# Angles kept in SBUF until a sine pass in every third step: re-ordering a tuned recurrence-and-mixer kernel

## The chip, the cores and the metric

One core of a Trainium2 chip runs the whole program. The metric is the device time of one execution in microseconds (us). Before the change the kernel took 284.85 us, the median of 3 runs (280.71 to 285.94). A run that is more than 1.5% above the fastest of its kernel is called slow; 285.94 is one. Ratios here are of fast runs only.

The engines are named as in the profile: PE is TensorE's matmuls, PEld its weight loads, DVE is VectorE, ACT is ScalarE, POOL is GpSimd. In the traces each has its own sequence of instructions, with waits where an input is missing.

## The reference, cut to what matters

The first half is a linear recurrence with decay over 768 time steps, for 4 batches and 8 heads of 40. The second half is a mixer: angles theta, sine and cosine, a product with two 768x768 token weights, and a channel layer.

```python
for t in range(S):                                   # B, H, S, D = 4, 8, 768, 40
    y[:, :, t] = einsum('bhd,bhde->bhe', rt, state)
    Sa = einsum('bhde,bhe->bhd', state, at)
    state = state * wt[:, :, None, :] - einsum('bhd,bhe->bhde', Sa, bt) \
            + einsum('bhd,bhe->bhde', vt, kt)
x = y.transpose(0, 2, 1, 3).reshape(B, S, 320)

theta = x @ w_theta                                  # 320 x 320
zr, zi = x * cos(theta), x * sin(theta)
y = einsum('ts,bsd->btd', w_tok_r, zr) + einsum('ts,bsd->btd', w_tok_i, zi)
u = x + y
out = u + maximum(u @ w_ch, 0)
```

## The kernel before

The sequence is cut into 24 tiles of 128 time steps (4 batches of 6). One pass of the main loop is one **step**. It does the recurrence of tile i, prepares tile i+2, finishes tile i-1, and does one mixer row of an earlier batch. Names that return below:

- **nx** is the negated intermediate of the recurrence. ScalarE copies it once per step, so the times of the 24 nx copies cut the run into steps. "Nx 8" is the start of the ninth copy.
- **lw, invW, Wi** are a logarithm and two exponentials on ScalarE. They prepare a tile.
- **kb** is the **key product** (k and b times invW), **ah** is a times Wi, **rv** the casts of r and v. All three are on GpSimd, and TensorE then transposes them.
- **aT, rvT, kbT, nuT, gd, xT, uT** are copies of transposes from PSUM to SBUF.
- **z products** are x times cosine and x times sine, six per sine pass, on GpSimd.

```python
def prep_csi(i):
    ...                                              # matmul of the running log-decay
    nc.scalar.activation(out=q.invW..., in_=csi[:, 0:DM], func=AF.Exp)
    nc.gpsimd.tensor_tensor(out=q.kbh[:, :, :, 0:D], in0=q.kb,
                            in1=q.invW.to_broadcast([128, 2, H, D]), op=ALU.mult)

def prep_rv(i):
    for j in range(2):
        nc.gpsimd.tensor_copy(out=q.rvb[:, j, :, 0:D], in_=q.rv[:, j])

def moe_phase(bi, js):                               # three tiles at once
    th = tile_of(ps_sc, [128, 1024], FP32, "sc")     # one of two large PSUM buffers
    ...                                              # theta = xT * w_theta, into th
    for c in range(2):                               # cosine (bias pi/2), then sine
        tc.keep_in_program_order(nc.scalar.activation(
            out=cs[:, c, 0:n * DM], in_=th[:, 0:n * DM], func=AF.Sin,
            bias=(pi2_col[:, :], 0.0)[c]))
    ...                                              # 6 z products on GpSimd

for i in range(N):                                   # N = 24
    nxt(load, i + 4)
    nxt(prep_ln, i + 2)
    rec_x0(i)                                        # makes nx
    nxt(tr_a, i + 1)                                 # makes aT
    ...
    nxt(prep_csi, i + 2)
    rec_nu(i)
    if i > 0: out_y(i - 1)
    nxt(sc_psiphi, i + 1)                            # scores from aT and kbT
    ...
    nxt(prep_cse, i + 2)
    if i > 0: out_xt(i - 1)                          # makes xT
    nxt(prep_rv, i + 2)
    for m in yrows: moe_y(*m)                        # one mixer row
    nxt(tr_rv, i + 2); nxt(tr_kb, i + 2)
    ...
    if i < NCH: moe_wtok(i)                          # token weights, steps 0 to 5
    if i == 1: moe_weights()
    if ci == 3: moe_phase(bi, (0, 1, 2)); ln_exp_again()
    if ci == 0 and bi > 0: moe_phase(bi - 1, (3, 4, 5)); ln_exp_again()
```

In the trace each of the seven sine passes in the loop has two table loads on ScalarE, one ahead of its sines and one behind them (1.28 us each, see below; `ln_exp_again` is the second). The framework's scheduler may move any instruction that is not given to `keep_in_program_order`, so the order in the trace is not the order of this text.

## Time and profile before

| part of the run, cut by nx | us | what it is |
|---|---|---|
| start to nx 0 | 25.4 | first loads, first tiles prepared |
| nx 0 to nx 8 | 78.8 | the inputs come in |
| nx 8 to nx 23 | 143.1 | steady: 10 plain steps, 5 with a sine pass |
| nx 23 to the end | 35.5 | tail |

First, lines of the profile's page: span, busy time per engine, then the busy share of 40 equal slices of the span in tenths (PEclk is the granted clock of TensorE in tenths), and the DMA packets.

```profile
span 282.8 us, 8177 instructions
PE 219.1 (77%) x3392; PEld 174.1 (62%) x3392; DVE 183.1 (65%) x262; ACT 159.6 (56%) x294; POOL 125.2 (44%) x172
...
PEclk9999999888779999998998899979997999999979
DMA  8999999899399849827963597457410000011012
...
DMA packets 155684, 30.81 MB, mean 109 GB/s; under 512 B 150400, under 2 KB 155648, under 8 KB 155648
```

No engine is full over the whole span, so the average names no limit; the parts have to be read one by one. The DMA line shows one limit: the 16 engines are busy through the first slices. Nearly all packets are under 512 B (a head's row of 40 floats is 160 B), and the next view has all engines busy at 160 to 170 GB/s. That the size of the packets is the cause is not shown.

The windows view of the kernel before, one line per part (the input-bound part in two). Columns: window, length, busy us with number of instructions for PE, PEld, DVE, ACT, POOL, then granted clock, DMA share (1.00 is 16 busy engines), GB/s.

```profile
0.00:25.40 25.40, 8.83 (x87) 6.59 (x88) 14.57 (x43) 7.04 (x13) 12.32 (x27) 1.00 0.97 160
25.40:66.20 40.80, 31.21 (x512) 25.67 (x512) 27.74 (x35) 23.61 (x45) 19.27 (x29) 0.96 1.04 170
66.20:104.20 38.00, 26.93 (x492) 22.79 (x492) 25.17 (x31) 22.80 (x43) 23.15 (x31) 0.87 0.77 133
104.20:247.30 143.10, 126.34 (x2077) 102.14 (x2076) 104.20 (x133) 96.51 (x179) 65.87 (x81) 0.95 0.49 92
247.30:282.80 35.50, 25.78 (x229) 16.92 (x227) 11.40 (x22) 9.62 (x19) 4.57 (x6) 0.95 0.13 47
```

In the steady part PE is busy 126.34 of 143.10 us, 88%. Most of the other 12% (16.8 us) is a wait for ScalarE: 11.9 us, in the waits view further down. This is the timeline of ACT around one sine pass (start, duration, engine, line, operation, then idle time before it and what ended that):

```profile
119.69 0.46 ACT L255 ACTIVATE nx<-sm 128x320 bf16<-128x320 f32 x1
120.16 1.28 ACT L405 ACT_TABLE_LOAD   x1
121.46 1.06 ACT L405 ACTIVATE cs<-sc,pi_col 128x960 f32<-128x960 f32 x1
122.42 0.96 ACT L405 ACTIVATE cs<-sc 128x960 f32<-128x960 f32 x1
123.40 1.28 ACT L414 ACT_TABLE_LOAD   x1
124.69 0.58 ACT L182 COPY aT<-sm 128x512 bf16<-128x512 bf16 x1
```

The pass takes 4.5 us, from 120.16 to 124.69, and it stands between nx and aT. TensorE's scores need aT. All table loads of the sine passes in this trace took 1.28 us, and the first sine here starts 0.02 us after its load (120.16 + 1.28 = 121.44, start 121.46).

The second kind of hole is in the input-bound part. The timeline of POOL before, in step 4 to 5, which took 15.5 us:

```profile
70.77 0.45 POOL L126 CAST rv_104<-raw_rv 128x320 bf16<-128x320 f32 x1 [5.74 <-DMA raw_rv<-in_r_dram]
71.18 0.78 POOL L410 TENSOR_TENSOR zr<-cs,x_118 128x320 bf16<-128x320 f32 x1
...
74.92 0.78 POOL L410 TENSOR_TENSOR zi<-cs,x_122 128x320 bf16<-128x320 f32 x1
75.67 1.52 POOL L137 TENSOR_TENSOR kb_98<-raw_kb,invW 128x640 bf16<-128x640 f32 x1
```

GpSimd waits 5.74 us for a transfer of r, then does six z products, and only then the key product. Two lines of the waits view of before (engine, line, what it waited for: total us, times, longest) show what both holes cost TensorE (of the second line, the 6.2 are this hole; the rest is a wait in step 0):

```profile
PE sc L196 <- ACT aT L182: 11.9, 5, 2.7
...
PE sm L164 <- POOL kb_98 L137: 8.5, 2, 6.2
```

### The profile page before, as it was taken

Reading aid. Unit: us, or ns where it says so; the run is one execution under the profiler, and the core shown is the slowest. Engines: PE = TensorE matmul, PEld = TensorE weight load, DVE = VectorE, ACT = ScalarE, POOL = GpSimd, SP = SyncE. Lnnn points to the kernel's source line nnn. Section 1 sums busy time; section 2 is a strip of 40 time slices with the busy share of each in tenths; the row PEclk is TensorE's granted clock in tenths of the full one; section 3 lists DMA queues with packets and bytes.
Section 4 is the critical chain, followed back from the end, with each engine's and each line's share of the span. In section 5 each row is a group of like instructions: output and inputs, shape, how many; then the busy total and the mean of one; then the engine's idle time right before and its main releaser. Section 6 shows DMA issues by size and latency. Waiting matters only on the chain.

```text
span 282.8 us, 8177 instructions
## 1 busy us (share of the span) xinstructions
PE 219.1 (77%) x3392; PEld 174.1 (62%) x3392; DVE 183.1 (65%) x262; ACT 159.6 (56%) x294; POOL 125.2 (44%) x172
## 2 busy tenths in 40 slices
PE   1374698686198779969996999699969995996693
PEld 0253577475087667857775788477757875764462
DVE  7643579694069869846884788468846885752042
ACT  3243366377237986685658666956595569334121
POOL 3742546521954484464446444564445333204200
PEclk9999999888779999998998899979997999999979
DMA  8999999899399849827963597457410000011012
GB/s 136 179 182 155 189 181 161 148 170 176 65 171 166 150 77 172 158 57 123 175 123 77 96 167 140 92 94 143 87 32 2 26 26 26 1 49 49 0 46 93
DMA packets 155684, 30.81 MB, mean 109 GB/s; under 512 B 150400, under 2 KB 155648, under 8 KB 155648
## 3 DMA queue, kind: packets, MB, share of 16 engines
q1 hardware_dynamic: 153216, 27.54, 53.5%
q0 software_dynamic: 2432, 2.77, 6.2%
q8 instruction: 26, 0.43, 0.6%
q14 instruction: 10, 0.08, 0.1%
HBM read 29.13 MB, written 3.93 MB: 117 GB/s over the span
## 4 chain that ended last, share of the span: by engine, by line
PE 51%; ACT 14%; DMA 10%; DVE 8%; SPq 7%; POOL 4%; issue 4%; POOLq 0%; ACTq 0%; DVEq 0%
PE sm L420 13%; PE sm L164 9%; SPq L115 7%; DMA raw_rv<-in_r_dram 7%; PE sc L196 7%; PE sm L382 4%; ACT cs L405 3%; ACT L414 3%; DVE lamv L204 3%; PE sc L382 3%; DMA raw_rv<-in_v_dram 2%; PE sm L344 2%; PE sm L285 2%; ACT aT L182 2%; PE sc L420 2%
## 5 line engine op out<-in xcount | busy, mean ns | idle before, releaser
L204 DVE TENSOR_TENSOR psi<-sc,mask_p 128x1024 bf16<-128x1024 f32 x24 | 29.2, 1218 | 17.3 <-PE sc L196 17.3
L190 ACT COPY rvT<-sm 128x1024 bf16<-128x1024 bf16 x24 | 24.3, 1013 | 21.2 <-PE sm L164 21.2
L420 PE MATMUL sm<-zr,wtok_r 128*128 128x320 bf16 x120 | 36.0, 320 | 0.0
L420 PE MATMUL sm<-zi,wtok_i 128*128 128x320 bf16 x120 | 35.5, 316 | 0.0
L175 DVE COPY kbT<-sm 128x1024 bf16<-128x1024 bf16 x24 | 16.6, 690 | 22.4 <-PE sm L164 22.4
L204 DVE TENSOR_TENSOR phi<-sc,mask_n 128x1024 bf16<-128x1024 f32 x24 | 29.2, 1215 | 0.5 <-PE sc L196 0.5
L196 PE MATMUL sc<-aT,kbT 64*128 64x128 bf16 x384 | 19.0, 235 | 13.2 <-ACT aT L182 11.9
L204 DVE TENSOR_TENSOR lamu<-sc,mask_p 128x1024 bf16<-128x1024 f32 x24 | 29.2, 1215 | 0.0
L204 DVE TENSOR_TENSOR lamv<-sc,mask_p 128x1024 bf16<-128x1024 f32 x24 | 29.2, 1215 | 0.0
L313 ACT COPY nuT<-sm 128x512 bf16<-128x512 bf16 x24 | 14.0, 585 | 24.3 <-PE sm L164 24.3
L196 PEld LDWEIGHTS <-kbT 64*128 64x128 bf16 x384 | 13.5, 102 | 14.7 <-issue 13.5
L420 PEld LDWEIGHTS <-wtok_r 128*128 128x128 bf16 x144 | 15.0, 104 | 10.7 <-issue 4.9
L304 ACT COPY gd<-sm 128x320 bf16<-128x320 bf16 x20 | 8.5, 426 | 19.1 <-PE sm L164 19.1
L420 PEld LDWEIGHTS <-wtok_i 128*128 128x128 bf16 x144 | 14.9, 103 | 7.0 <-issue 1.2
L347 ACT COPY uT<-sm 128x384 bf16<-128x384 bf16 x24 | 11.4, 483 | 12.7 <-PE sm L344 12.7
L182 ACT COPY aT<-sm 128x512 bf16<-128x512 bf16 x24 | 14.2, 593 | 3.8 <-PE sm L164 3.7
L382 PE MATMUL sm<-wch,uT 128*128 128x320 bf16 x72 | 14.4, 315 | 2.3 <-ACT uT L347 2.3
L263 PEld LDWEIGHTS <-phi 128*128 128x128 bf16 x192 | 8.6, 97 | 11.7 <-issue 10.1
L255 ACT ACTIVATE nx<-sm 128x320 bf16<-128x320 f32 x24 | 10.8, 450 | 6.2 <-PE sm L251 6.2
L331 PEld LDWEIGHTS <-lamu 128*128 128x128 bf16 x192 | 13.1, 97 | 1.7 <-DVE lamu L204 0.7
L328 PEld LDWEIGHTS <-lamv 128*128 128x128 bf16 x192 | 13.8, 96 | 0.4 <-issue 0.4
L137 POOL TENSOR_TENSOR kb_100<-raw_kb,invW 128x640 bf16<-128x640 f32 x6 | 9.2, 1541 | 10.8 <-ACT invW L134 10.8
(324 smaller groups left out, 676.0 us busy)
## 6 DMA issues: line engine op xcount, KB each, us to landing
raw_w<-in_w_dram SPq DMA_DIRECT2D x24, 160.0 KB, 4.4
raw_kb<-in_k_dram SPq DMA_DIRECT2D x24, 160.0 KB, 3.2
raw_kb<-in_b_dram SPq DMA_DIRECT2D x24, 160.0 KB, 3.7
raw_a<-in_a_dram SPq DMA_DIRECT2D x24, 160.0 KB, 3.8
raw_rv<-in_r_dram SPq DMA_DIRECT2D x24, 160.0 KB, 4.0
raw_rv<-in_v_dram SPq DMA_DIRECT2D x24, 160.0 KB, 4.5
out_dram<-oo SPq DMA_DIRECT2D x24, 160.0 KB, 1.8
wtok_row<-in_moe_w_tok_r_dram POOLq DMA_DIRECT2D x6, 192.0 KB, 4.8
```

The lines of the kernel that those rows point to most:

```text
L115: nc.sync.dma_start(out=dst, in_=src(ap))
L164: nc.tensor.transpose(out=dst[:, g * 128:(g + 1) * 128], in_=src[:, 2 * g:2 * g + 2, :].rearrange("p a b -> p (a b)"), identity=ident)
L175: nc.vector.tensor_copy(out=q.kbT.rearrange("p a b -> p (a b)"), in_=pt)
L182: nc.scalar.copy(out=q.aT, in_=pt[:, 0:512])
L190: nc.scalar.copy(out=q.rvT.rearrange("p a b -> p (a b)"), in_=pt)
L196: nc.tensor.matmul(P[:, p, g, :], lhsT=lhs[rows(p), g * 128:(g + 1) * 128], rhs=rhs[rows(p), g * 128:(g + 1) * 128], start=True, stop=True)
L204: nc.vector.tensor_tensor(out=s.rearrange("p a b c -> p (a b) c"), in0=P.rearrange("p a b c -> p (a b) c"), in1=mask.to_broadcast([128, 2 ...
L313: nc.scalar.copy(out=q.nuT, in_=pt[:, 0:512])
L328: nc.tensor.matmul(o, lhsT=q.lamv[:, p, g, :], rhs=q.kbh[:, 0, h, 0:D], start=first, stop=False, skip_group_check=True)
L331: nc.tensor.matmul(o, lhsT=q.lamu[:, p, g, :], rhs=q.kbh[:, 1, h, 0:D], start=False, stop=True, skip_group_check=True)
L382: nc.tensor.matmul(dst, lhsT=lhs[:, kt, :], rhs=rhs[:, kt, :], start=kt == 0, stop=kt == 2)
L420: nc.tensor.matmul(yp, lhsT=wtok[nm][:, sb, j * 128:(j + 1) * 128], rhs=z[:, sb], start=start and n == 0, stop=stop and n == 2 * len(sbs) - 1)
```

## The change

The intent: theta goes to SBUF by a small copy in every step, so a sine pass no longer holds a large PSUM buffer and can stand where ScalarE has time, behind xT. In those steps the three copies that follow (rvT, gd, uT) go to VectorE. Z products come one step after their sines. The mixer's weight loads are taken out of the start and their transposes come two steps later. The first two tiles are prepared on ScalarE and VectorE instead of GpSimd. The logarithm runs three tiles ahead instead of two.

```diff
     def prep_ln(i):
-        nc.scalar.activation(out=q.lw[:, :, 0:D], in_=q.w, func=AF.Ln)
+        tc.keep_in_program_order(
+            nc.scalar.activation(out=q.lw[:, :, 0:D], in_=q.w, func=AF.Ln))
     def prep_rv(i):
         for j in range(2):
-            nc.gpsimd.tensor_copy(out=q.rvb[:, j, :, 0:D], in_=q.rv[:, j])
+            if i < 2:
+                nc.scalar.copy(out=q.rvb[:, j, :, 0:D], in_=q.rv[:, j])
+            else:
+                nc.gpsimd.tensor_copy(out=q.rvb[:, j, :, 0:D], in_=q.rv[:, j])
     def prep_csi(i):
-        nc.gpsimd.tensor_tensor(out=q.kbh[:, :, :, 0:D], in0=q.kb,
-                                in1=q.invW.to_broadcast([128, 2, H, D]),
-                                op=ALU.mult)
+        for j in range(2):
+            (nc.vector if i < 2 else nc.gpsimd).tensor_tensor(
+                out=q.kbh[:, j, :, 0:D], in0=q.kb[:, j], in1=q.invW[:, 0],
+                op=ALU.mult)
     # ... the a product likewise; copies of rvT, gd, xT and uT become
+    def evac(out, in_):
+        if busy_act[0]:
+            nc.vector.tensor_copy(out=out, in_=in_)
+        else:
+            nc.scalar.copy(out=out, in_=in_)
     # ... moe_phase is cut into three
+    def moe_theta(i):
+        tp = tile_of(ps_sm, [128, 512], FP32, "sm")
+        mix3(tp[:, 0:DM], tiles[i].xT, wth)
+        nc.scalar.copy(out=ths[bi][:, j], in_=tp[:, 0:DM])
+    # moe_z: the six z products;  moe_sines: the two sines, from ths in SBUF
     for i in range(N):
         nxt(load, i + 4)
-        nxt(prep_ln, i + 2)
         rec_x0(i)
         nxt(tr_a, i + 1)
+        if i > 1:
+            moe_theta(i - 2)
     # ...
         if i > 0:
             out_xt(i - 1)
+        due = None
+        if sines:
+            due = (bi, (0, 1, 2)) if ci == 4 else (bi - 1, (3, 4, 5))
+            moe_sines(*due)
+            ln_exp_again()
+            busy_act[0] = True
         nxt(prep_rv, i + 2)
     # ... mixer row, transposes, rec_gd, uT
+        busy_act[0] = False
+        if i == 0:
+            moe_weights()
         if i < NCH:
-            moe_wtok(i)
-        if i == 1:
-            moe_weights()
-        if ci == 3:
-            moe_phase(bi, (0, 1, 2)); ln_exp_again()
-        if ci == 0 and bi > 0:
-            moe_phase(bi - 1, (3, 4, 5)); ln_exp_again()
+            wtok_load(i)
+        if 2 <= i < NCH + 2:
+            wtok_trans(i - 2)
+        nxt(prep_ln, i + 3)
+        if z_due:
+            moe_z(*z_due)
+        z_due = due
```

(Shortened: padding is zeroed in another order, the work ahead of the loop is re-ordered, the weight loads are pinned in program order, mixer rows start one step later and catch up with two rows in each of the last three steps, and the tail uses the new pieces.)

More of the change, by code (lines that the diff above doesn't have):

```diff
@@ L62, with padded, last24 @@
     NB = 4
-    def padded(name, shape, n):
-        ts = []
-        for i in range(n):
-            t = consts.tile(shape, BF16, name=f"{name}_{i}")
-            nc.vector.memset(t, 0.0)
-            ts.append(t)
-        return ts
-    lw_t = padded("lw", [128, H, 64], 2)
-    ah_t = padded("ah", [128, H, 64], 2)
-    kb_t = padded("kb", [128, 2, H, 64], NB)
-    rv_t = padded("rv", [128, 2, H, 64], NB)
-    nu_t = padded("nu", [128, H, 64], 2)
-    gt_t = padded("gt", [128, G, 2, 64], 2)
-    x_t = padded("x", [128, 3 * 128], 2 * NCH)
-    u_t = padded("u", [128, 3 * 128], 3)
+    def padded(name, shape, n, pads):
+        ts = [consts.tile(shape, BF16, name=f"{name}_{i}") for i in range(n)]
+        for i, t in enumerate(ts):
+            to_zero.append((i, pads(t)))
+        return ts
+    to_zero = []
+    def last24(t):
+        return t[:, :, D:64] if len(t.shape) == 3 else t[:, :, :, D:64]
+    lw_t = padded("lw", [128, H, 64], 2, last24)
+    ah_t = padded("ah", [128, H, 64], 2, last24)
+    kb_t = padded("kb", [128, 2, H, 64], NB, last24)
+    rv_t = padded("rv", [128, 2, H, 64], NB, last24)
+    nu_t = padded("nu", [128, H, 64], 2, last24)
+    gt_t = padded("gt", [128, G, 2, 64], 2, last24)
+    x_t = padded("x", [128, 3 * 128], 2 * NCH, lambda t: t[:, DM:])
+    u_t = padded("u", [128, 3 * 128], 3, lambda t: t[:, DM:])
+    for i, t in sorted(to_zero, key=lambda e: e[0]):
+        nc.vector.memset(t, 0.0)
     raw = ctx.enter_context(tc.tile_pool(name="raw", bufs=3))
@@ L90 @@
     ps_sm = ctx.enter_context(tc.tile_pool(name="ps_sm", bufs=4, space=PSUM))
+    busy_act = [False]
+    def evac(out, in_):
[3 more added lines that the diff above has]
+            nc.scalar.copy(out=out, in_=in_)
     def rows(p):
@@ L157, in prep_cse @@
         q.ah = ah_t[i % 2]
-        nc.gpsimd.tensor_tensor(out=q.ah[:, :, 0:D], in0=q.a,
-                                in1=q.Wi[:, 0:DM].rearrange("p (h d) -> p h d", h=H),
-                                op=ALU.mult)
+        (nc.vector if i < 2 else nc.gpsimd).tensor_tensor(
+            out=q.ah[:, :, 0:D], in0=q.a,
+            in1=q.Wi[:, 0:DM].rearrange("p (h d) -> p h d", h=H), op=ALU.mult)
     def transpose4(dst, src):
@@ L189, in tr_rv @@
         q.rvT = tile_of(trs, [128, 2, 512], BF16, "rvT")
-        nc.scalar.copy(out=q.rvT.rearrange("p a b -> p (a b)"), in_=pt)
+        evac(out=q.rvT.rearrange("p a b -> p (a b)"), in_=pt)
     def score(lhs, rhs):
@@ L303, in rec_gd @@
         gd = tile_of(sml, [128, 8, D], BF16, "gd")
-        nc.scalar.copy(out=gd, in_=pt[:, 0:512].rearrange(
+        evac(out=gd, in_=pt[:, 0:512].rearrange(
             "p (n d) -> p n d", d=64)[:, :, 0:D])
@@ L346, in x_transpose @@
         dst = tile_of(xp, [128, 3, 128], BF16, tag)
-        nc.scalar.copy(out=dst.rearrange("p a b -> p (a b)"), in_=pt[:, 0:384])
+        evac(out=dst.rearrange("p a b -> p (a b)"), in_=pt[:, 0:384])
         return dst
@@ L354, with pool_dma, wtok_load, wtok_trans @@
     wtok = {}
+    def pool_dma(out, in_):
+        tc.keep_in_program_order(nc.gpsimd.dma_start(out=out, in_=in_))
     def moe_weights():
         for dst, src in ((wth, moe_w_theta), (wch, moe_w_ch)):
-            nc.gpsimd.dma_start(out=dst[:, 0:2, :], in_=src[0:256, :].rearrange(
+            pool_dma(out=dst[:, 0:2, :], in_=src[0:256, :].rearrange(
                 "(a p) d -> p a d", p=128))
-            nc.gpsimd.dma_start(out=dst[0:64, 2, :], in_=src[256:320, :])
+            pool_dma(out=dst[0:64, 2, :], in_=src[256:320, :])
     for nm in ("r", "i"):
         wtok[nm] = mw.tile([128, NT, S], BF16, name=f"wtok_{nm}")
-    def moe_wtok(tb):
+    wrow = ctx.enter_context(tc.tile_pool(name="wrow", bufs=3))
+    wrows = {}
+    def wtok_load(tb):
         for nm, ap in (("r", moe_w_tok_r), ("i", moe_w_tok_i)):
-            row = tile_of(mk, [128, S], BF16, "wtok_row")
-            nc.gpsimd.dma_start(out=row, in_=ap[tb * 128:(tb + 1) * 128, :])
+            row = tile_of(wrow, [128, S], BF16, f"wtok_row_{nm}")
+            pool_dma(out=row, in_=ap[tb * 128:(tb + 1) * 128, :])
+            wrows[nm, tb] = row
+    def wtok_trans(tb):
+        for nm in ("r", "i"):
             pt = tile_of(ps_sm, [128, 1024], BF16, "sm")
@@ L371, in moe_wtok @@
                 nc.tensor.transpose(out=pt[:, sb * 128:(sb + 1) * 128],
-                                    in_=row[:, sb * 128:(sb + 1) * 128],
+                                    in_=wrows[nm, tb][:, sb * 128:(sb + 1) * 128],
                                     identity=ident)
@@ L385, with moe_z, moe_sines @@
     zs = {}
-    def moe_phase(bi, js):
+    ths = {}
+    def moe_theta(i):
+        bi, j = divmod(i, NCH)
+        if bi not in ths:
+            ths[bi] = tile_of(mk, [128, NT, DM], FP32, "th")
+        tp = tile_of(ps_sm, [128, 512], FP32, "sm")
+        mix3(tp[:, 0:DM], tiles[i].xT, wth)
+        nc.scalar.copy(out=ths[bi][:, j], in_=tp[:, 0:DM])
+    cs_of = {}
+    def moe_z(bi, js):
+        cs = cs_of[bi, js[0]]
+        for m, j in enumerate(js):
+            for c in range(2):
+                nc.gpsimd.tensor_tensor(out=zs[bi][c][:, j], in0=cs[:, c, m],
+                                        in1=tiles[bi * NCH + j].x, op=ALU.mult)
+    def moe_sines(bi, js):
         if bi not in zs:
@@ L391, in moe_phase @@
                       tile_of(mk, [128, NT, DM], BF16, "zi"))
-        zr, zi = zs[bi]
-        n = len(js)
-        if n > 1:
-            th = tile_of(ps_sc, [128, 1024], FP32, "sc")
-        else:
-            th = tile_of(ps_sm, [128, 512], FP32, "sm")
-        for m, j in enumerate(js):
-            lo, hi = m * DM, m * DM + DM
-            cuts = [lo, 512, hi] if lo < 512 < hi else [lo, hi]
-            for c0, c1 in zip(cuts, cuts[1:]):
-                mix3(th[:, c0:c1], tiles[bi * NCH + j].xT, wth[:, :, c0 - lo:c1 - lo])
-        cs = tile_of(mk, [128, 2, 3 * DM], FP32, "cs")
+        j0, n = js[0], len(js)
+        cs = tile_of(mk, [128, 2, 3, DM], FP32, "cs")
+        cs_of[bi, j0] = cs
         for c in range(2):
             tc.keep_in_program_order(nc.scalar.activation(
-                out=cs[:, c, 0:n * DM], in_=th[:, 0:n * DM], func=AF.Sin,
+                out=cs[:, c, 0:n], in_=ths[bi][:, j0:j0 + n], func=AF.Sin,
                 bias=(pi2_col[:, :], 0.0)[c]))
-        for c, z in enumerate((zr, zi)):
-            for m, j in enumerate(js):
-                nc.gpsimd.tensor_tensor(out=z[:, j], in0=cs[:, c, m * DM:m * DM + DM],
-                                        in1=tiles[bi * NCH + j].x, op=ALU.mult)
     def ln_exp_again():
@@ L453, in nxt @@
             f(i)
-    def prep(i):
-        prep_ln(i)
-        prep_csi(i)
-        prep_cse(i)
     rows_at = {}
-    for s in range(NCH + 2, 3 * NCH + 2):
-        rows_at[s] = [divmod(s - NCH - 2, NCH)]
-    for s, js in ((20, (0,)), (21, (1,)), (22, (2, 3)), (23, (4, 5))):
-        rows_at[s] = [(2, j) for j in js]
+    for s in range(NCH + 3, 3 * NCH + 3):
+        rows_at[s] = [divmod(s - NCH - 3, NCH)]
+    for s in range(3):
+        rows_at[3 * NCH + 3 + s] = [(2, 2 * s), (2, 2 * s + 1)]
     for i in range(4):
         load(i)
-    prep(0)
+    prep_ln(0)
+    prep_csi(0)
+    prep_cse(0)
     tr_kb(0)
     tr_a(0)
-    prep_rv(0)
-    prep(1)
     sc_psiphi(0)
     ev_phi(0)
+    prep_rv(0)
     tr_rv(0)
+    prep_ln(1)
+    prep_csi(1)
+    prep_cse(1)
     lv = score(tiles[0].rvT[:, 1], tiles[0].rvT[:, 0])
     tiles[0].lamv = masked("lamv", lv, mask_p)
+    tr_kb(1)
     prep_rv(1)
-    tr_kb(1)
     tr_rv(1)
+    prep_ln(2)
     prev = []
+    z_due = None
     for i in range(N):
+        bi, ci = divmod(i, NCH)
         yrows = rows_at.get(i, [])
+        sines = ci == 4 or (ci == 1 and bi > 0)
         nxt(load, i + 4)
-        nxt(prep_ln, i + 2)
         rec_x0(i)
         nxt(tr_a, i + 1)
-        for m in prev:
-            moe_ch(*m)
+        if i > 1:
+            moe_theta(i - 2)
         nxt(prep_csi, i + 2)
@@ L493 @@
             out_y(i - 1)
+        nxt(prep_cse, i + 2)
         nxt(sc_psiphi, i + 1)
@@ L497 @@
         nxt(ev_phi, i + 1)
-        nxt(prep_cse, i + 2)
         if i > 0:
             out_xt(i - 1)
+        due = None
[4 more added lines that the diff above has]
+            busy_act[0] = True
+        for m in prev:
+            moe_ch(*m)
         nxt(prep_rv, i + 2)
@@ L509 @@
             moe_ut(*m)
+        busy_act[0] = False
+        if i == 0:
+            moe_weights()
         if i < NCH:
-            moe_wtok(i)
-        if i == 1:
-            moe_weights()
-        bi, ci = divmod(i, NCH)
-        if ci == 3:
-            moe_phase(bi, (0, 1, 2))
-            ln_exp_again()
-        if ci == 0 and bi > 0:
-            moe_phase(bi - 1, (3, 4, 5))
-            ln_exp_again()
+            wtok_load(i)
[5 more added lines that the diff above has]
+        z_due = due
         prev = yrows
+    moe_theta(N - 2)
+    moe_sines(B - 1, (3, 4))
+    moe_z(B - 1, (3, 4))
+    out_y(N - 1)
     for m in prev:
         moe_ch(*m)
-    moe_phase(B - 1, (3, 4))
-    out_y(N - 1)
     acc = [tile_of(ps_sc, [128, 2, 512], FP32, "sc") for _ in range(2)]
@@ L532 @@
         y_part(yps[j], B - 1, j, range(NT - 1), True, False)
-    moe_phase(B - 1, (5,))
+    moe_theta(N - 1)
+    moe_sines(B - 1, (5,))
+    moe_z(B - 1, (5,))
     for j in range(NT):
```

## The prediction

> **What bounds the kernel now.** 284.85 us (profiled span 282.8). Cut by the start of the negated-x copy (nx) on ScalarE, one per step, the run has four parts.
>
> 1. Start, to 25.4 us (timeline): the first nx stands behind the logarithm of tile 3, which waited 5.3 us for its input (25.0).
> 2. Input-bound part, nx 0 (25.4) to nx 8 (104.3). The windows view gives 16 DMA engines fully busy at 167 GB/s up to 70 us; 150,400 of 155,684 packets are under 512 B. [...] A tile is 0.98 MB, mixer rows 0.39 MB a step: about 8.1 us a step while both load, 5.9 after (estimates). Two steps take 13.9 and 15.5 us: the first holds a sine pass (61.0 to 66.1); in the second GpSimd has a cast of r, waiting 5.7 us for DMA, then six z products (4.7 us), ahead of the key product, for which TensorE and VectorE wait 7.5 us.
> 3. Steady part, nx 8 to nx 23 (247.3): plain steps 7.2 to 8.1 us, sine steps 12.5 to 13.4. Groups of three take about 28.7 us; TensorE is busy 25.3 to 25.8 of it. A sine pass is load 1.28 + sines 1.06 and 0.96 + load 1.28 = 4.6 us on ScalarE, between nx and aT, and TensorE's scores wait for aT (up to 2.7 us, waits view).
> 4. Tail, 35.5 us.
>
> [...]
>
> **The change.**
> - As many table loads. Added: 24 theta copies on ScalarE, 0.44 us each (estimate from equal-sized copies). Theta drops from 12 matmuls to 9 per three tiles and frees the large PSUM buffer.
> - The pass moves behind xT, where the rvT, gd and uT copies (1.01 + 0.43 + 0.48) go to VectorE in those steps. ScalarE's order gives nx to xT 4.5 + 0.44 + pass 4.6 + logarithm 0.48 = 10.0 us for a sine step. VectorE: 7.5 us in a plain step, about 9.0 in a sine step. Groups of 8 + 8 + 10 = 26 us, near TensorE's floor of 25.
> - z products come a step later, off the key product's way.
> - Weights are issued after the first tiles: 0.8 MB, about 4.5 us of DMA, leaves the first 20 us. Tiles 0 and 1 avoid GpSimd; tile 0's scores precede tile 1's transposes; the logarithm three tiles ahead follows gd. Nx 0 near 19.
>
> **Sum.** Start -6. Input-bound part: nx 1 near 26, then about 8 us a step with two sine steps of 10: nx 8 near 84 to 86 instead of 104.3, -19 in all by then. Steady: 15 steps in 130 instead of 143, -13. Tail: +0 to +1 (a theta copy in the last chain). Span near 251.
>
> **Predicted 253 us, 80% range 244 to 265.** Faster by over 2%: 0.95; within 2%: 0.04; slower: 0.01.
>
> **Right if:** first nx by 20 us; no step over 11 us after step 1; sine steps 9.5 to 10.5; TensorE's wait for aT at passes gone; the 7.5 us waits for a key product gone; tail 35 to 37.
>
> **Wrong if:** VectorE bounds sine steps (over 11 us); GpSimd's z products still delay keys; the theta copy stretches plain steps above 8.3; input DMA, with weights in steps 0 to 5, holds steps at 9 or more; or the granted clock falls below 0.94 [...].

The cuts are two passages and a clause that no run of this case shows. No term of the sum is among them: -19 by nx 8 (the -6 of the start included), -13 and 0 to +1 take the span from 282.8 to about 251, and the 2 us by which the 284.85 us exceed their span make it 253. Two figures in it are estimates. The 4.5 us of DMA for 0.8 MB of weights (also in the expectation of e9) would be 4.8 at the 167 GB/s that it names. The 7.5 and 9.0 us for VectorE were not measured either: in the windows view VectorE was busy 5.9 to 7.3 us in the plain steps of the steady part before, and 6.4 and 8.1 us in a plain and a sine step of the kernel after (118.0 to 126.4 and 109.1 to 118.0).

## The result, and the profile after

The kernel after took 260.64 us, the median of 4 fast runs (260.36 to 262.26). The kernel before had 283.58 (280.71 to 285.94, 4 runs); without the slow run, which is 1.9% above the lowest, the median of three is 282.30. The ratio of fast runs is 0.923, with a 95% interval of 0.914 to 0.933: faster. A ratio is the mean time of one kernel's fast runs over that of the other's of the same rounds, so it is not quite the ratio of the medians quoted.

| part, cut by nx | before | predicted | after |
|---|---|---|---|
| start to nx 0 | 25.4 | 19 | 18.7 |
| nx 0 to nx 8 | 78.8 | 65 to 67 | 74.4 |
| nx 8 to nx 23 | 143.1 | 130 | 130.3 |
| tail | 35.5 | 35.5 to 36.5 | 37.1 |
| profiled span | 282.8 | about 251 | 260.5 |

One row is off by 8 us. It is nearly the whole difference between 253 predicted and 260.6.

Lines of the page of the kernel after, the same as shown of before:

```profile
span 260.5 us, 8110 instructions
PE 215.0 (83%) x3368; PEld 167.8 (64%) x3368; DVE 185.4 (71%) x287; ACT 160.4 (62%) x303; POOL 120.9 (46%) x186
...
PEclk9999997999659979999999999999999999999778
DMA  7999999999999898767697579645500001011012
...
DMA packets 155685, 30.81 MB, mean 118 GB/s; under 512 B 150401, under 2 KB 155649, under 8 KB 155649
```

All busy shares are up because nearly the same work is done in less time. The granted clock is lowest in slices 11 and 12, at 6 and 5 tenths (the slow step below), and it is 7, 7, 8 at the end (the tail).

The windows view of the kernel after, columns as before. The third line is the step from nx 5 (61.0) to nx 6 (75.75).

```profile
0.00:18.70 18.70, 8.01 (x86) 6.66 (x87) 10.99 (x49) 8.09 (x15) 1.86 (x12) 1.00 1.05 165
18.70:61.00 42.30, 35.12 (x613) 28.06 (x613) 32.57 (x40) 28.20 (x56) 24.86 (x39) 0.96 1.01 171
61.00:75.75 14.75, 7.81 (x121) 6.15 (x121) 6.85 (x9) 4.67 (x12) 10.47 (x17) 0.70 1.07 179
75.75:93.10 17.35, 14.22 (x267) 11.38 (x266) 14.95 (x22) 13.85 (x24) 9.46 (x15) 0.96 1.02 163
93.10:223.40 130.30, 122.72 (x2060) 97.90 (x2060) 107.42 (x146) 94.82 (x181) 67.83 (x97) 0.99 0.55 102
223.40:260.50 37.10, 27.12 (x226) 17.61 (x225) 12.62 (x26) 10.82 (x21) 6.41 (x9) 0.87 0.13 45
```

In the steady part PE is now busy 122.72 of 130.30 us, 94% against 88%. As the profile models the ends of matmuls, this is no distance to a peak. It says that less waiting is left. The windows also show DMA fully busy up to nx 8 (share 1.01 to 1.07, at 163 to 179 GB/s); the busy work before that point is not what fills the time (PE is busy 65.16 of those 93.1 us).

The timeline of ACT after, around one sine pass in the steady part:

```profile
109.07 0.44 ACT L273 ACTIVATE nx<-sm 128x320 bf16<-128x320 f32 x1
...
112.54 0.48 ACT L103 COPY xT_2435<-sm 128x384 bf16<-128x384 bf16 x1
113.04 1.28 ACT L443 ACT_TABLE_LOAD   x1
114.33 1.10 ACT L443 ACTIVATE cs<-th,pi_col 128x960 f32<-128x960 f32 x1
115.34 0.99 ACT L443 ACTIVATE cs<-th 128x960 f32<-128x960 f32 x1
116.34 1.28 ACT L447 ACT_TABLE_LOAD   x1
117.63 0.47 ACT L134 ACTIVATE lw_87<-raw_w 128x320 bf16<-128x320 f32 x1
118.01 0.42 ACT L273 ACTIVATE nx<-sm 128x320 bf16<-128x320 f32 x1
```

The step is 118.01 - 109.07 = 8.9 us: 3.5 from nx to xT, 0.5 for xT, 4.6 for the pass, 0.4 for the logarithm. The first sine starts 0.01 us after its table load (113.04 + 1.28 = 114.32, start 114.33). ScalarE is without a gap from xT to the next nx, yet TensorE loses less than before, because aT is long done. It still waits for the nx behind the pass, up to 1.4 us (waits view below).

The timeline of POOL after, in the slow step, and the ScalarE line that ends it:

```profile
61.28 0.45 POOL L143 CAST rv_97<-raw_rv 128x320 bf16<-128x320 f32 x1 [2.92 <-DMA raw_rv<-in_r_dram]
...
63.63 0.82 POOL L432 TENSOR_TENSOR zr<-cs,x_102 128x320 bf16<-128x320 f32 x1
...
67.38 0.78 POOL L432 TENSOR_TENSOR zi<-cs,x_104 128x320 bf16<-128x320 f32 x1
69.47 0.45 POOL L143 CAST rv_94<-raw_rv 128x320 bf16<-128x320 f32 x1 [1.31 <-DMA raw_rv<-in_r_dram]
...
70.52 1.67 POOL L155 TENSOR_TENSOR kb_93<-raw_kb,invW 128x320 bf16<-128x320 f32 x2
```

```profile
75.75 0.44 ACT L273 ACTIVATE nx<-sm 128x320 bf16<-128x320 f32 x1 [8.98 <-PE sm L269]
```

The key product of tile 7 (70.52) had its invW at 62.9 us. It stood behind six z products and behind two casts of tile 8, whose r arrived only at 69.5. In the program's text this key product comes ahead of those casts and of those z products; the scheduler put it behind both. Of the two, the casts came last: the z products ended at 68.16, and GpSimd then still waited 1.31 us for r, whose transfer had been issued at 62.82, before the first of them. So the z products alone did not set the start of the key product in this step; the input did, for an engine that had been given a cast of tile 8 ahead of the key product of tile 7. Of the waits view of after, the lines of TensorE for this and for nx:

```profile
PE sm L182 <- POOL kb_93 L155: 6.5, 2, 6.3
...
PE sm L410 <- ACT nx L273: 7.5, 9, 1.4
```

Before, the longest wait of this kind in the input-bound part was 6.2 us. So the wait that the change was to remove has come back one step later. The line for aT, 11.9 us before, has no counterpart any more; waits for nx in the steady part, 5.9 us of the 7.5, are about half as long.

### The profile page after: what moved, and what is told of

It reads as the page before. It is cut to its first block, busy times and chain, and to the rows that moved or that the text cites. A ratio compares the mean times of both kernels' runs of the same rounds, so it can differ in the third digit from the quotient of the medians.

```text
span 260.5 us, 8110 instructions
## 1 busy us (share of the span) xinstructions
PE 215.0 (83%) x3368; PEld 167.8 (64%) x3368; DVE 185.4 (71%) x287; ACT 160.4 (62%) x303; POOL 120.9 (46%) x186
## 4 chain that ended last, share of the span: by engine, by line
PE 46%; ACT 15%; issue 12%; DMA 10%; POOL 9%; DVE 4%; SPq 3%; POOLq 0%; DVEq 0%; ACTq 0%
PE sm L453 10%; DMA raw_rv<-in_r_dram 9%; PE sm L182 7%; PE sc L214 6%; PE sm L410 5%; ACT cs L443 4%; SPq L128 3%; ACT L443 2%; ACT L447 2%; PE sc L453 2%; PE sm L362 2%; PE sm L349 2%; PE sm L278 2%; DVE lamu L222 1%; POOL kb_93 L155 1%
## 5 line engine op out<-in xcount | busy, mean ns | idle before, releaser
L103 ACT COPY rvT<-sm 128x1024 bf16<-128x1024 bf16 x18 | 18.2, 1013 | 26.0 <-PE sm L182 26.0
L453 PE MATMUL sm<-zr,wtok_r 128*128 128x320 bf16 x120 | 33.8, 304 | 0.0
L453 PE MATMUL sm<-zi,wtok_i 128*128 128x320 bf16 x120 | 33.7, 303 | 0.0
L453 PEld LDWEIGHTS <-wtok_r 128*128 128x128 bf16 x144 | 14.4, 100 | 9.6 <-issue 3.9
L273 ACT ACTIVATE nx<-sm 128x320 bf16<-128x320 f32 x24 | 10.4, 432 | 11.5 <-PE sm L269 11.5
L103 ACT COPY uT<-sm 128x384 bf16<-128x384 bf16 x18 | 8.5, 483 | 14.1 <-PE sm L362 14.1
L143 POOL CAST rv_96<-raw_rv 128x320 bf16<-128x320 f32 x12 | 5.4, 453 | 24.5 <-DMA raw_rv<-in_r_dram 21.8
L155 POOL TENSOR_TENSOR kb_93<-raw_kb,invW 128x320 bf16<-128x320 f32 x12 | 10.1, 866 | 13.2 <-ACT invW L151 13.2
L424 ACT COPY th<-sm 128x320 f32<-128x320 f32 x24 | 10.6, 441 | 8.6 <-PE sm L410 8.6
L155 POOL TENSOR_TENSOR kb_91<-raw_kb,invW 128x320 bf16<-128x320 f32 x10 | 8.4, 861 | 14.4 <-ACT invW L151 14.4
L174 ACT ACTIVATE Wi<-sm 128x328 f32<-128x328 f32 x24 | 10.7, 448 | 5.9 <-PE sm L168 3.1
L214 PEld LDWEIGHTS <-kbT 64*128 64x128 bf16 x384 | 11.9, 99 | 3.7 <-issue 2.9
```

Of the source, the lines that this page charges most:

```text
L103: nc.scalar.copy(out=out, in_=in_)
L155: (nc.vector if i < 2 else nc.gpsimd).tensor_tensor(out=q.kbh[:, j, :, 0:D], in0=q.kb[:, j], in1=q.invW[:, 0], op=ALU.mult)
L174: nc.scalar.activation(out=q.Wi, in_=cse[:, 0:DM + 8], func=AF.Exp)
L214: nc.tensor.matmul(P[:, p, g, :], lhsT=lhs[rows(p), g * 128:(g + 1) * 128], rhs=rhs[rows(p), g * 128:(g + 1) * 128], start=True, stop=True)
L453: nc.tensor.matmul(yp, lhsT=wtok[nm][:, sb, j * 128:(j + 1) * 128], rhs=z[:, sb], start=start and n == 0, stop=stop and n == 2 * len(sbs) - 1)
```

## The experiments

Theory A: the missing 8 us of the input-bound part come from the order on GpSimd, where the key product stands behind casts that wait for DMA and behind z products. Rival B: input DMA itself holds those steps, with the token weights in steps 0 to 5 taking part of it. Rival C: the steady part or the added theta copies. Further runs undo single parts of the change to see what each is worth.

Several runs of the kernel before were slow (about 283 to 286 against 279 to 283). All ten experiment kernels gave correct results. Kernels of different calls ran on different chips, so differences of about 1 us between calls are not read.

### e1_pool_order: GpSimd pinned to the order of the text

```diff
+    def pin(i, ins):
+        if i >= 2:
+            tc.keep_in_program_order(ins)
     # around: key products, a products, casts of r and v, z products
-            (nc.vector if i < 2 else nc.gpsimd).tensor_tensor(
+            pin(i, (nc.vector if i < 2 else nc.gpsimd).tensor_tensor(
```

> The changed kernel with GpSimd's key products, a products, r/v casts and z products pinned in program order, the same DMA bytes at the same places. Theory A (the stall between nx 5 and nx 6, 14.8 us, comes from GpSimd's order: six z products of 4.7 us and a cast of the next tile's r that waits for DMA stand ahead of the key product of tile 7): nx 6 moves from 75.8 to about 69, nx 8 from 93.1 to 86 to 88, the wait of TensorE for that key product (6.3 us) goes, total about 254. Theory B (the stall is input DMA alone, 167 GB/s with 2.8 MB of weights in the first six steps): total within 1% of the changed kernel, 259 to 262, the wait only changes its name. Both: nx 3 stays near 43.7, because rv of tile 4 lands only at about 38.

Measured: 254.63 us (253.37 to 257.03), ratio 0.905 (0.898 to 0.913). Nx 8 came at 86.5 instead of 93.1. The step from nx 5 to nx 6 went from 14.8 to 7.9 us. The timeline of POOL of this kernel, the same place:

```profile
60.29 1.69 POOL L160 TENSOR_TENSOR kb<-raw_kb,invW 128x320 bf16<-128x320 f32 x2 [5.27 <-ACT invW L156]
61.95 0.85 POOL L181 TENSOR_TENSOR ah<-raw_a,Wi 128x320 bf16<-128x320 f32 x1
62.75 0.83 POOL L148 CAST rv<-raw_rv 128x320 bf16<-128x320 f32 x2
...
64.66 0.82 POOL L438 TENSOR_TENSOR zr<-cs,x 128x320 bf16<-128x320 f32 x1
...
68.43 0.78 POOL L438 TENSOR_TENSOR zi<-cs,x 128x320 bf16<-128x320 f32 x1
```

Nothing but the pins on GpSimd's work was edited, and 6.6 us of the 8 are back by nx 8. Theory A is shown for that part: in the six kernels that keep the scheduler's order, the early token weights and the place of the pass (the kernel after, e4, e5, e8, e9, e10), nx 8 comes at 90.9 to 93.6 and the step from nx 5 takes 12.3 to 15.3 us; in the two pinned ones with early token weights (e1, e6), nx 8 comes at 86.5 and 87.1 and that step takes 7.9 and 9.2. One thing I had not expected: the step from nx 2 to nx 3 also fell, from 11.5 to 8.0. In the kernel after, a cast on GpSimd had waited there 5.79 us for r, ahead of a key product (36.8 us); pinned, the key product of that stretch was done at 34.1 to 35.8. How much of that is the order is open: nx 3 came at 40.4 in e1 and at 42.1 in e6, which has the same text up to there. The steady part is the same 130.3 us in both.

### e2_wtok_late: token weights six steps later

```diff
-        if i < NCH:
-            wtok_load(i)
-        if 2 <= i < NCH + 2:
-            wtok_trans(i - 2)
+        if 6 <= i < NCH + 6:
+            wtok_load(i - 6)
+        if 8 <= i < NCH + 8:
+            wtok_trans(i - 8)
```

> The changed kernel with the loads and transposes of the token-mixing weights (2.4 MB) six steps later, each still before the row that reads it; GpSimd's order left to the scheduler (z products still ahead of the key product of tile 7). Theory B (DMA bytes): nx 3 near 40, nx 6 at 64 to 67, nx 8 at 82 to 85, total 250 to 253. Theory A (order): z products still delay the key product, nx 5 to nx 6 stays over 11 us, total 256 or more. In both the late transposes may add up to 1 us per step to steps 8 to 13, as TensorE is busy 94% there.

Measured: 257.99 us (256.93 to 259.20), ratio 0.917 (0.911 to 0.922). Nx 8 came at 77.7, 15.4 us earlier than in the kernel after; the plain steps from nx 2 to nx 7 took 6.3 to 6.7 us. Nx 8 to nx 23 then took 141.9 us instead of 130.3. So rival B is right in its part: the token weights do hold the first steps. Their 6 x 0.39 MB at 171 GB/s are about 13.8 us (an estimate from the windows view and the tensors' sizes). But 11.6 of the 15.4 us are given back. One step of 15.3 us (nx 10 to nx 11) is among them. In it the key product of tile 12 (106.57) stands behind a cast of tile 14 that waits 6.06 us for a transfer, and the z products come only later (109.83): the same hole, without z products ahead, in the steps that now load the token weights.

Neither list of expected numbers fits as a whole: nx 6 (60.9) and nx 8 came earlier than B had them, the total is above B's 253, and the step from nx 5 to nx 6, which A had above 11 us, took 6.3. The trace shows why: z products again stand ahead of the key product of tile 7, but this time the scheduler put the casts of tile 8 behind it: it starts at 57.63, they at 59.25, and TensorE waits 1.1 us for it. So z products ahead of a key product do not make the hole by themselves. It also means that this run moved the bytes and, unasked, the order; e3 keeps them apart.

### e3_both: pinned order and late token weights

The edit is e1's and e2's together.

> Both edits together. If A and B are two separate losses: nx 6 at 60 to 63, nx 8 at 79 to 82, total 246 to 250. If either edit alone already removes the whole stall: no better than the better of the two, within 1%.

Measured: 256.05 us (253.75 to 256.65), ratio 0.908 (0.901 to 0.915). The 15.3-us step fell to 11.0, but nx 8 to nx 23 still took 136.1 us, 5.8 more than in e1. Six steps carry the transposes and copies of the token weights there, so about 1 us each on average. A likely reason is that TensorE has little time to spare in that part, while in the input-bound part it waits anyway (in e1's windows it is busy 121.92 of 130.30 us in the one, 54.61 of 68.0 us in the other). Nx 6 (65.4), nx 8 (82.9) and the total are all above what was expected of two separate losses. Against e1, which has the same pinned order, nx 8 came 3.6 us earlier: that is about what the later bytes alone bring by then. It came later than in e2; what the pinned order costs there was not looked into. On top of the pinned order, late token weights bring nothing that these runs show: 256.05 against 254.63, with ranges that overlap.

### e4_start_undone: first two tiles back on GpSimd

```diff
-            if i < 2:
+            if i < 0:
     # likewise in the key product and the a product
```

> The changed kernel with tiles 0 and 1 prepared on GpSimd again (casts, key and a products), all else kept. My account (the start gained from weights out of the way and from the order: tile 0's scores ahead of tile 1, the logarithm of tile 3 behind gd; and what comes after waits for input DMA): nx 0 at 19.5 to 21.5 instead of 18.7, the difference gone by nx 3 (43 to 44), total within 1%, 259 to 263. Rival (moving the two tiles off GpSimd is what moved the start): nx 0 at 23 to 25 and 4 to 6 us longer in all, 265 or more.

Measured: 258.64 us (258.44 to 260.14). Nx 0 came at 19.9 instead of 18.7, nx 3 at 41.9 (earlier than the 43 to 44 expected), and nx 8 at 93.1, as in the kernel after. Keeping the first tiles off GpSimd brings 1.2 us at nx 0 and nothing later.

### e9_weights_early: the weight loads back in the start

```diff
     for i in range(4):
         load(i)
+    moe_weights()
+    wtok_load(0)
     # ... in the loop
-        if i == 0:
-            moe_weights()
-        if i < NCH:
+        if 0 < i < NCH:
             wtok_load(i)
```

> The changed kernel with the theta and channel weights and the first token-mixing rows (0.8 MB) issued before the first tile is prepared, as the kernel before did; all later weights as in the changed kernel. My account (0.8 MB is 4.5 us of DMA at the start, but the same bytes are wanted before tile 4 anyway): nx 0 at 20 to 23 instead of 18.7, nx 3 within 1.5 us of 43.7, nx 8 within 2 us of 93, total within 1% of 260.6. Rival (the spread of the weights is worth its 4.5 us in the total): 264 to 266.

Measured: 261.94 us (261.38 to 262.01), ratio 0.928 (0.922 to 0.934). Nx 0 came at 23.7, 5.0 us later than in the kernel after and beyond the 20 to 23 expected. (The trace has all these loads issued by 7.6 us; in the kernel before the scheduler had spread them from 2.5 to 25.5 us, so this is an earlier issue than before, not the same.) Nx 3 came at 44.1 against 43.7, and nx 8 at 93.6 against 93.1. A start 5 us earlier is gone after three steps. The likely reason is that the loads were moved, not removed, and the same bytes have to arrive before the same step.

### e10_start_as_before: e9, and the logarithm of tile 3 ahead of the loop

```diff
+    prep_ln(3)                    # ahead of the loop
     # ... in the loop
-        nxt(prep_ln, i + 3)
+        if i > 0:
+            nxt(prep_ln, i + 3)
```

> The same, and the logarithm of tile 3 ahead of nx 0 on ScalarE, as in the kernel before. My account (both together, not the engine of tiles 0 and 1, made the 6.7 us of the start): nx 0 at 23.5 to 26, standing behind that logarithm, and in the total at most 2 us more than the changed kernel, because input DMA decides the arrival at nx 3: 260 to 263. Rival (the late start is carried to the end): 266 to 268.

Measured: 260.49 us (259.81 to 261.32), ratio 0.924 (0.916 to 0.932), nx 0 at 21.2 and nx 8 at 92.0. The edit did not do what it was made for: nx is not pinned, and the scheduler put nx 0 ahead of the logarithm of tile 3. The expectation for nx 0 failed for that reason, so the run does not test the late logarithm of the kernel before. It only shows once more that 2.5 us at nx 0 leave the total where it was.

### e5_no_dve_evac: rvT, gd and uT stay on ScalarE

```diff
-            busy_act[0] = True
```

> The changed kernel with the rvT, gd and uT copies of the sine steps left on ScalarE. My account (ScalarE's in-order path nx, xT, sine pass, logarithm sets the sine step): 1.9 us more on ScalarE in each of 7 sine steps, sine steps from 8.9 to about 10.8, total 8 to 13 us longer, 269 to 273, of which some is absorbed by plain steps becoming shorter. Rival (TensorE, 94% busy, sets the groups of three, and the copies are beside the point): groups of three stay within 0.5 us of 26.0, total within 1%.

Measured: 266.55 us (265.08 to 269.03), ratio 0.948 (0.940 to 0.956). In the steady part, four of the five sine steps took 10.4 to 10.5 us instead of 8.8 to 8.9 (the last one 9.3), and three of the plain steps behind them were 0.5 to 0.8 us shorter (7.1 to 7.5 instead of 7.6 to 8.3). Moving the copies is worth 6 us. I had expected 8 to 13: the sign was right and the size was not, as those plain steps take a part back.

The copies also cost less on VectorE. From the trace of the kernel after, a 128x1024 bf16 copy out of PSUM (rvT) took 0.688 us there and 1.013 us on ScalarE, and a 128x384 one (uT) 0.347 and 0.483 us.

### e7_pass_behind_nx: the sine pass back between nx and aT

```diff
         rec_x0(i)
-        nxt(tr_a, i + 1)
+        due = None
+        if sines:
+            due = (bi, (0, 1, 2)) if ci == 4 else (bi - 1, (3, 4, 5))
+            moe_sines(*due)
+            ln_exp_again()
+        nxt(tr_a, i + 1)          # its copy aT is pinned in program order
     # ... nothing in the old place but
+            busy_act[0] = True
```

> The changed kernel with the sine pass put back between nx and the aT copy (angles still from SBUF, rvT, gd and uT still on VectorE in those steps). My account (the place of the pass is most of the steady gain: there TensorE's scores, and all that follows in the step, wait for aT behind 4.6 us): sine steps 11.5 to 12.5 instead of 8.9, 5 sine steps in nx 8 to nx 23, that part 143 to 148 instead of 130, total 275 to 282. Rival (ScalarE's total work per group counts, not its place): groups of three stay at 26 to 26.5, total within 1.5% of 260.6.

Measured: 297.35 us (295.99 to 298.98), slower than the kernel before. I had expected 275 to 282, so this missed. Sine steps took 12.6 to 18.6 us, and nx 8 to nx 23 took 160.1. The waits view of this kernel has the line that the change had removed:

```profile
PE sc L214 <- ACT aT L200: 27.5, 7, 4.5
```

So the place of the pass matters: with it put back, the kernel loses 36.7 us, more than the whole change had gained. How much of the gain is due to the place alone can't be read from this run, as it ends up worse than before, where aT also waited behind the pass. Part of that is in the waits view: in the steady part TensorE waits 22.1 us for aT in five passes, against 11.9 before, which is 10.2 us of the 17.0 by which that part is longer. The kernel before had other work for TensorE there (the channel layer of the previous row stood between nx and xT; the change moved it behind xT). VectorE waits up to 4.8 us for the scores, up to 2.5 before, and the three copies it was given stand behind them in its order. No run separates these.

### e8_theta_twice: the theta copy done a second time

```diff
         nc.scalar.copy(out=ths[bi][:, j], in_=tp[:, 0:DM])
+        nc.scalar.copy(out=ths[bi][:, j], in_=tp[:, 0:DM])
```

> The changed kernel with every theta copy on ScalarE done twice (24 more copies of 0.44 us, same values). If the copy lies on the path in all steps: 0.44 us more per step from nx 8 on (6.6 us over 15 steps) and 0.9 in the tail, 7 to 8 us, total 268. If it only counts where ScalarE's order sets the pace, in the sine steps, and in the tail: 7 x 0.44 + 0.9 = 4 us, total 264 to 265. If it is hidden: within 0.5%, up to 262.

Measured: 261.96 us (260.54 to 263.57); nx 8 to nx 23 took 130.7 us, against 130.3. Twenty-four more copies of 0.44 us each are hidden. Rival C falls, and so does the idea that the theta copy makes plain steps longer than predicted. One thing that changed in them is that theta's three matmuls, about 0.41 us of TensorE (an estimate: three times the 0.136 us from one start to the next in the trace of the kernel after), now stand in every step, where there had been twelve with each pass; 8.0 + 0.41 agrees with the 8.3 to 8.5 seen. That is arithmetic, not a run.

### e6_z_spread: e1, with the z products given out over two or three steps

```diff
-    def moe_z(bi, js):
+    def moe_z(bi, js, ms=(0, 1, 2)):        # and skips tiles not in ms
     # ... in the loop
-        if z_due:
-            moe_z(*z_due)
-        z_due = due
+        if due:
+            z_due = [(due, (0,)), (due, (1,)), (due, (2,))] if ci == 4 else [
+                (due, (0,)), (due, (1, 2))]
+        if z_due:
+            (zb, zj), ms = z_due.pop(0)
+            moe_z(zb, zj, ms)
```

> The pinned GpSimd order (254.6 us) with the z products of one sine pass given out over two or three steps instead of six in a row, so that one key product stands behind at most 1.6 us of them (3.1 once) instead of 4.7. If the burst of six is what is left of the stall there (nx 6 to nx 7 took 10.7 us with the key product starting 1.7 us after its turn): that step at 8.5 to 9.2, total 252.5 to 253.5. If input DMA takes over at once: unchanged within 0.5%, 253.5 to 256.

Measured: 253.37 us (251.66 to 254.86). All four runs are below the lowest of the kernel after and of the kernel before. Nx 8 came at 87.1, no earlier than in e1 (86.5), and the steady part was again 130.4. The step from nx 6 to nx 7 fell from 10.7 to 8.3, as expected of the burst of six, and the total lies at the edge of both expectations; but nx 2 to nx 3 (10.3 against 8.0) and nx 5 to nx 6 (9.2 against 7.9) were longer. The runs overlap with those of e1, so the spreading itself is not shown to bring anything in the total. The runs of e1, e2, e3 and e6 all lie below the lowest of the kernel after; e1 and e6 have the lowest medians.

## Why the prediction was right or wrong, point by point

The class (faster) and the range (244 to 265) held. The middle was 7.6 us too low, and the sum tells where.

**Steady part, predicted 130 us, measured 130.3.** The mechanism was right: the pass behind xT ends TensorE's wait for aT (11.9 us before, none after). E7 shows that this place matters, and e5 that the copies on VectorE do. That the sum fits to 0.3 us is luck: its composition was off and cancelled: sine steps took 8.8 to 8.9 instead of 10.0, because ScalarE went from nx to xT in 3.5 us instead of 4.5 plus a theta copy; plain steps took mostly 8.3 to 8.5 instead of 8.0 (7.6 to 10.0 over all ten).

**Input-bound part, predicted nx 8 at 84 to 86, measured 93.1.** This is the term that was mis-sized, by about 8 us. The step that failed is "z products come a step later, off the key product's way", and with it "the 7.5 us waits for a key product gone" and "no step over 11 us after step 1" (11.5 and 14.8 were seen). A step later they met the next key product. But they were not even what held it last: that was the cast of tile 8, which waited for r until 69.47, after the z products had ended. The prediction had seen such a cast in the kernel before (5.7 us of waiting for DMA), and the change did nothing about it. The order on GpSimd was left to the scheduler, as before, and I had taken the order of the text for that of the engine. No run moves only the casts or only the z products; e2, where the z products stayed ahead and the casts of tile 8 did not, took 6.3 us for that step. What stood ahead on GpSimd shows in the trace: the key product had its inputs at 62.9 and began at 70.52, behind all of it. With the order pinned, nx 8 is at 86.5 and the total at 254.6 us.

The prediction named the failure among what would make it wrong ("GpSimd's z products still delay keys"), and also input DMA. E2 shows the second as a real limit, and also that putting the token weights off is largely paid back later (11.6 of 15.4 us).

**Start, predicted nx 0 near 19, measured 18.7.** The number was right and its use in the sum was not. E9 starts 5 us later and ends at most 1.3 us later (261.94 against 260.64, in different calls); e4 starts 1.2 us later and ends no later. In these runs, with input DMA full up to nx 8 (share 1.01 to 1.07 in the kernel after), an earlier start was not a gain of its own. The 11.1 us won by nx 8 belong to that part as a whole; I did not split them further.

**Tail, predicted 0 to +1, measured +1.6.** Theta copies of 0.42 to 0.45 us stand ahead of the two last sine passes, as foreseen. The rest seems to go with a lower granted clock in that stretch, 0.87 against 0.95. In e1, whose tail is nearly the same text, it lasted 36.0 us at a clock of 0.95. (In the other experiments it lasted 34.8 to 36.5 us, and 37.6 in e8 with its doubled theta copies.) So at the clock of before the new tail was 0.5 us longer than its 35.5 in e1, within what was predicted, and the rest of the 1.6 stands beside the lower clock; no run set the clock. What lowers it is not shown: in the kernel after it was 0.70 in the step with the long TensorE wait and 0.99 in the steady part, but 1.00 in the start, where PE is busy for only 8.01 of 18.70 us.

## What to carry to other kernels

In the kernel after, a key product on GpSimd began 7.6 us after its inputs were there (62.9, 70.52), behind a cast on the same engine that waited for a transfer, and with the order pinned nx 8 came 6.6 us earlier. So look for transfers awaited by an off-path engine just ahead of its urgent work; write that order down with pins where a scheduler would choose it, and read it from the trace, not from the text. In the part of this kernel that is bound by input transfers an earlier start was worth next to nothing (nx 0 came 5.0 us earlier than in e9, the end 1.3 us), while the token weights' transposes cost about 1 us a step in the part where TensorE was 94% busy: keep such work out of there. A sine pass with its two table loads did best here where the copies that other engines wait for were already done (260.64 us, against 297.35 with the pass ahead of aT), with the copies just behind it on another engine (266.55 with them on ScalarE).
